# Sparse attention ahead of two routed expert layers: keys on two load queues, the last batch's pooled units ahead of its tiles, a shorter chain behind the last tiles, and first products around the late routing

## The chip, the cores and the metric

One core of a Trainium2 chip. The metric is the device time of one execution in microseconds, the median of several runs. TensorE multiplies, VectorE and ScalarE work on elements, GpSimd fills, adds and issues indirect transfers, SyncE issues plain transfers. In the rows they are PE (PEld: its weight loads), DVE, ACT, POOL and SP; SPq and ACTq are the instructions with which SyncE and ScalarE issue a transfer into their own load queue.

## What is computed

Three stages in a row, all in float32. Attention over 4 batches, 8 heads, 576 positions, head width 64, as the sum of a pooled and a local part:

```python
q_d = q.reshape(B, H, Sd, factor, D).mean(axis=3)          # factor 4; k_d, v_d alike
out_up = np.repeat(sm_attn(q_d, k_d, v_d), factor, axis=2)
mask = np.abs(pos[:, None] - pos[None, :]) < factor        # a band of 7 positions
out_local = np.matmul(softmax(where(mask, scale * q @ k.T, -1e9)), v)
return out_up + out_local
```

Its 2,304 tokens of 512 go through a layer of 8 experts with one expert per token. A skip score decides which tokens are computed (`x @ w_skip > 0`), argmax of `x @ w_gate` picks the expert, and the result is `x + gate * relu(x @ w1[e]) @ w2[e]`. A second layer of 8 experts then takes the two best experts of noisy logits for each token.

## The kernel before

**Layout.** Attention works on 18 tiles of 128 tokens (4.5 per batch, all heads at once). Of a batch's keys one half of the head width lies on partitions 0 to 63 and the other on 64 to 127, `kT[128, 4, 2, S]`, with zeros in the places between, so that one product serves two heads. `load_qk` loads the two halves by two transfers of 64 partitions each and then the queries (128 partitions), all in SyncE's queue. Batch 0 comes in two pieces (positions 0 to 191 for tile 0, then the rest). `load_local` loads a tile's window of values, `vw`, by two transfers of 48 partitions; four window buffers take turns. `load_v` loads a batch's values for pooling.

**Steps.** `push` emits one step of a software pipeline. A step's unit is a local tile (`Local`) or one of five pooled units of a batch (`Pooled`; unit 4 comes first). A step emits the unit's scores and softmax, the transposes (`turn`) of the unit two steps back, then fill work that was scheduled for this step, then the products with the values of the unit three steps back. After these the window of the tile four later is asked for, since its buffer is free. `POOLED` and `PATTERN` say after which tile a batch's pooled units stand: for batch 3 units 4, 0, 1 after tile 12 and units 2, 3 after tile 13.

**The chain behind a tile.** When a batch's pooled outputs are complete, its tiles are finished one per step (`finish`): `load_up` expands the pooled rows into `up` one step later (four buffers), `x_add` adds them to the tile's row `x` at step `ADD` = 3, `x_turn` transposes at `ADD + TURN` (+1), `x_part` multiplies with the routing weights at `ADD + PART` (+3), `x_logits` sums the parts at `ADD + LOGIT` (+5), puts the logits into `lg` and stores the row to `x_d`. Rows `x` have 8 buffers, so the values of tile 8 wait until the row of tile 0 is stored. Steps without a unit follow until the chain of tile 17 is through, 50 steps in all. Additions run on GpSimd, those of tiles 15 and 17 on VectorE.

**Routing of the first layer.** `routing_1(0, TA)` treats tiles 0 to 8 early, a few VectorE steps per `push` (`RS`); `early_2` gives the first expert its tokens, and `ahead1`, a block of 112 tokens of that expert, is gathered as soon as `GA` steps are emitted. `LA` and `LB` say when that expert's two weight matrices (2 MB each) may be asked for. `routing_1(TA, NT)`, the late routing, follows the last logits: counts (`pl.count`), VectorE steps, then `put_1`, a table by which the late tokens' indices are made. Meanwhile TensorE does ahead1's up products (`early_up`, 8 of them with 4 products each, order set by `UA` and `UC`) and, after the capacities, its down products (`ahead1.down`). Then the first block of the expert loop is turned (`ex1[0].turn`), all engines pass a branch, and the loop over experts begins.

**Order.** TensorE, VectorE, ScalarE and GpSimd run in the order in which the program emits their work (`manual_schedule`); SyncE's order in attention is set by a scheduler. In the profile every float32 product has two records on TensorE.

Of the kernel before, what the change touches and what calls it, by code (L numbers as in the profile page):

```python
# [10 lines left out]
F32 = mybir.dt.float32  # L11
# [75 lines left out]
POOLED = (3, 5, 9, 12)  # L87
# [11 lines left out]
def moe_attention_kernel(ctx, tc, q, k, v, w_skip, w_gate, w1, w2, g2, n2, noise, u1, u2, out, dbg=None):  # L99
# [497 lines left out]
    with ExitStack() as actx:  # L597
# [33 lines left out]
        def zero_keys(i, e0, e1, c0=0, c1=S):  # L631
            if c0 == 0:
                kTs.append(shared.tile([128, 4, 2, S], F32, name=f"kT{i}", bufs=1, tag=f"shared{i}"))
            t = kTs[i]
            fill(e0, t[0:64, :, 1, c0:c1])
            fill(e1, t[64:128, :, 0, c0:c1])
# [59 lines left out]
        for d in offsets[0:2]:  # L696
            distances(d)
        mask(offsets[0])
        zero_keys(0, V, P, 0, 192)
        mask(offsets[1])  # L700
        zero_exps(P)
        zero_values(A)
        zero_keys(0, A, P, 192, S)
        zero_exps(P)
        zero_values(A)
        zero_exps(P)
        zero_values(A)
        zero_pooled_keys(0, P, P)

# [12 lines left out]
        def start_2():  # L722
# [4 lines left out]
            nc.gpsimd.dma_start(x_d[0:1], kTs[1][0:1, 0, 1, 0:DM + 16])  # L727
            load_qk(1, 0, S)
# [11 lines left out]
        nc.vector.memset(wall, 0.0)  # L740
        fours = at.tile([128, 32], F32, name="fours", bufs=1)
        nc.vector.tensor_reduce(fours, ident.rearrange("p (c k) -> p c k", k=4), axis=AX.X, op=OP.add)
        nc.vector.tensor_reduce(sel, ident.rearrange("p (k c) -> p c k", k=4), axis=AX.X, op=OP.add)

        qT, qd, vgs, held = {}, {}, {}, {}

        def load_qk(b, c0, c1):

            held["k", b % 2] = b
            if c0 == 0:  # L750
                qT[b] = at.tile([128, 4, S], F32, name="qT", bufs=2)
            for g in range(2):
                r = slice(64 * g, 64 * g + 64)
                nc.sync.dma_start(kTs[b % 2][r, :, g, c0:c1], k[b, r, :, c0:c1])
            nc.sync.dma_start(qT[b][:, :, c0:c1], q[b, :, :, c0:c1])

        def pool_qk(b, n):
# [7 lines left out]
            if n >= 8 and b in ONDVE:  # L765
                for i in range(n - 8, 4, 3):
                    o, x = kd[64:128, i, 1], kT[64:128, i, 1]
                    nc.vector.tensor_reduce(o, x.rearrange("p (g r) -> p g r", r=4), axis=AX.X, op=OP.add)
            elif n < 8:
                i = n // 2  # L770
                o, x = (qd[b][:, i], qT[b][:, i]) if n % 2 == 0 else (kd[0:64, i, 0], kT[0:64, i, 0])
                nc.vector.tensor_reduce(o, x.rearrange("p (g r) -> p g r", r=4), axis=AX.X, op=OP.add)
            else:
                o, x = kd[64:128, :, 1], kT[64:128, :, 1].rearrange("p a (g r) -> p a g r", r=4)
# [141 lines left out]
        class Local:  # L916
# [6 lines left out]
            def scores(self):  # L923
# [5 lines left out]
                for i in range(4):  # L929
                    for s in range(4):  # L930
# [3 lines left out]
                                         kTs[b % 2][:, i, :, ks:ks + W], start=False, stop=True,  # L934
# [129 lines left out]
        def push(unit, *fill):  # L1064
# [46 lines left out]
        load_qk(0, 0, 192)  # L1111
        load_local(0)
        load_qk(0, 192, S)
        for t in range(1, 3):
            load_local(t)
        vgs[0] = load_v(0)

# [7 lines left out]
        for b in range(B):  # L1125
            for i, us in enumerate(PATTERN):
                pooled_after.setdefault(POOLED[b] + i, []).extend((b, u) for u in us)
        for t in range(NT):
            for b in range(B):
                if LOADQK[b] == t:  # L1130
                    load_qk(b, 0, S)
# [37 lines left out]
    run(early_up, UC)  # L1169
# [3 lines left out]
    run(early_up)  # L1173
# [380 lines left out]
    with ExitStack() as mctx:  # L1554
# [11 lines left out]
        ahead1.rooms["yT1"], ex1[0].rooms["xT1"] = (  # L1566
            xp.tile([128, KD, BLK1], F32, name=n, tag="rows2", bufs=5) for n in ("yT0", "xTb"))
# [322 lines left out]
```

## Time and profile before

| | before |
|---|---|
| runs shown | 812.48, 808.34, 814.06 us; median 812.48 |
| profiled execution | 809.09 us, its span 807.2 us |
| TensorE busy | 764.0 us, 95% of the span |
| VectorE, ScalarE, GpSimd busy | 357.1, 259.0, 236.0 us |
| granted TensorE clock, mean | 0.971 |
| moved by DMA | 131.55 MB, 163 GB/s on average |

A time is read in the profile as microseconds from the start of the span. An idle time stands in brackets behind a row of the timeline with what ended it. The granted clock is 1.00 at 2.4 GHz and 0.50 at 1.2 GHz.

### The profile page before, as it was taken

How to read it: one execution, taken by the hardware profiler on the slowest of the kernel's cores; microseconds unless marked ns; L12 is line 12 of the kernel's file. 1: busy time of each engine (PE TensorE's matmuls, PEld its weight loads, DVE VectorE, ACT ScalarE, POOL GpSimd, SP SyncE). 2: the span in 40 equal slices, each digit the busy share in tenths (PEclk: the TensorE clock that was granted, in tenths of full speed). 3: DMA queues.
4: the chain of work that ended last, by engine and by line, in shares of the span. 5: the costliest groups of instructions: out<-in, count | busy, mean ns of one | idle time of the engine just before them, and what ended most of it. 6: DMA issues, size and time to landing. Idle time of an engine off the chain costs nothing.

```text
span 807.2 us, 15233 instructions
## 1 busy us (share of the span) xinstructions
PE 764.0 (95%) x6265; PEld 674.4 (84%) x6265; DVE 357.1 (44%) x814; ACT 259.0 (32%) x492; POOL 236.0 (29%) x243
## 2 busy tenths in 40 slices
PE   4799898799999999998999999999999999999996
PEld 2467576699999999997899899898898898897984
DVE  3896767541111255545975434244243243243210
ACT  6245354211111204322333533234333343343211
POOL 8213513022022253303345502402404305102012
PEclk7999799599999999999999999999999999999999
DMA  9999565869888986234163843724625526424113
GB/s 228 274 260 249 146 172 134 290 160 364 300 304 283 336 312 206 75 87 79 64 170 124 211 128 116 168 80 119 157 67 164 108 83 166 109 79 68 18 14 47
DMA packets 64394, 131.55 MB, mean 163 GB/s; under 512 B 16145, under 2 KB 19232, under 8 KB 63424
## 3 DMA queue, kind: packets, MB, share of 16 engines
q1 hardware_dynamic: 36784, 64.95, 27.8%
q0 software_dynamic: 11984, 25.98, 15.9%
q10 hardware_dynamic: 15552, 39.59, 13.5%
q8 instruction: 52, 0.85, 0.4%
q14 instruction: 22, 0.18, 0.1%
HBM read 101.86 MB, written 23.91 MB: 156 GB/s over the span
## 4 chain that ended last, share of the span: by engine, by line
PE 71%; DMA 2%; issue 2%; DVE 1%; POOL 1%; ACT 0%; POOLq 0%; DVEq 0%; ACTq 0%; SPq 0%
PE pY L1544 26%; PE pH L1529 25%; PE pH L545 8%; PE pY L558 8%; PE pT L1514 2%; PE pT L577 1%; DMA nal<-l_d 1%; PE pT L524 1%; DMA rows<-x_d,ix2g 1%; DMA rows<-x_d,ixrg 1%; PE pT L335 1%; PE pH L566 0%; DMA l_d<-x,ix1w 0%; POOL out L306 0%; PE pH L582 0%
## 5 line engine op out<-in xcount | busy, mean ns | idle before, releaser
L1544 PE MATMUL pY<-w,hh 128*128 128x512 f32 (+6 forms) x640 | 201.0, 395 | 0.0
L1529 PE MATMUL pH<-xh,w 128*128 128x256 f32 (+7 forms) x1024 | 194.8, 302 | 0.0
L1529 PEld LDWEIGHTS pH<-xh,w 128*128 128x128 f32 x1024 | 162.3, 188 | 0.7
L1544 PEld LDWEIGHTS pY<-w,hh 128*128 128x128 f32 (+6 forms) x640 | 114.9, 183 | 26.9
L1205 DVE TENSOR_TENSOR w<-stg,w 128x1024 fp32r<-128x1024 f32 x64 | 82.8, 1299 | 106.7 <-ACT w L1204 106.4
L1544 PE MATMUL pY<-w,hl 128*128 128x512 f32 (+6 forms) x320 | 125.5, 392 | 0.0
L1529 PE MATMUL pH<-xl,w 128*128 128x256 f32 (+7 forms) x512 | 123.1, 301 | 0.0
L1534 DVE SCALAR_TENSOR_TENSOR hl<-pH,hh 128x256 fp32r<-128x256 f32 (+7 forms) x128 | 57.0, 474 | 129.0 <-ACT hh L1533 128.8
L306 POOL DMA_INDIRECT out<-yo,ix2w x35 | 67.6, 1933 | 129.1 <-ACT yo L1546 120.5
L1533 ACT ACTIVATE hh<-pH 128x256 fp32r<-128x256 f32 (+7 forms) x128 | 49.3, 424 | 149.4 <-PE pH L1529 145.5
L1529 PEld LDWEIGHTS pH<-xl,w 128*128 128x128 f32 x512 | 90.0, 188 | 0.0
L301 POOL DMA_INDIRECT rows<-x_d,ix2g x32 | 36.6, 1143 | 155.7 <-PE pT L1514 144.7
L1544 PEld LDWEIGHTS pY<-w,hl 128*128 128x128 f32 (+6 forms) x320 | 58.5, 183 | 15.3
L558 PE MATMUL pY<-hT,w 128*128 128x112 f32 (+7 forms) x512 | 70.9, 300 | 0.0
L1204 ACT ACTIVATE w<-stg 128x1024 fp32r<-128x1024 f32 x64 | 67.1, 1055 | 9.4 <-DMA stg<-in_moe_w 9.2
L558 PEld LDWEIGHTS pY<-hT,w 128*128 128x128 f32 x512 | 69.1, 195 | 0.2
L1546 ACT ACTIVATE yo<-pY,gt 128x512 f32<-128x512 f32 (+6 forms) x35 | 24.1, 688 | 136.7 <-PE pY L1544 76.1
L545 PE MATMUL pH<-xT,w 128*128 128x200 f32 (+6 forms) x448 | 66.2, 301 | 0.0
L545 PEld LDWEIGHTS pH<-xT,w 128*128 128x128 f32 x448 | 61.1, 190 | 1.8 <-issue 1.7
L306 POOL DMA_INDIRECT l_d<-x,ix1w x15 | 14.7, 983 | 92.7 <-DVE x L585 90.3
L560 DVE COPY yT<-pY 128x224 f32<-128x224 f32 (+7 forms) x16 | 7.5, 471 | 71.7 <-PE pY L558 71.7
L976 POOL TENSOR_TENSOR x<-x,up 128x512 f32<-128x512 f32 x16 | 20.2, 1276 | 57.6 <-DMA up<-od 28.4
(408 smaller groups left out, 861.2 us busy)
## 6 DMA issues: line engine op xcount, KB each, us to landing
w<-in_moe_w ACTq DMA_DIRECT2D x16, 2048.0 KB
stg<-in_moe_w SPq DMA_DIRECT2D x64, 512.0 KB, 3.4
vw<-in_v SPq DMA_DIRECT2D x36, 192.0 KB, 4.4
x_d<-x SPq DMA_DIRECT2D x18, 264.0 KB, 3.1
out<-zero ACTq DMA_DIRECT2D x3, 1536.0 KB, 8.5
v<-in_v SPq DMA_DIRECT2D x4, 1024.0 KB, 5.6
up<-od SPq DMA_DIRECT2D x14, 256.0 KB, 4.8
kT<-in_k SPq DMA_DIRECT2D x6, 576.0 KB
```

Source lines behind the costliest of these rows:

```text
L301: return nc.gpsimd.indirect_dma_start(out=dst, out_offset=None, in_=x_d[0:n + 1], in_offset=bass.IndirectOffsetOnAxis(ap=idx, axis=0))
L306: return nc.gpsimd.indirect_dma_start(out=dst, out_offset=bass.IndirectOffsetOnAxis(ap=idx, axis=0), in_=src, in_offset=None, **kw)
L545: nc.tensor.matmul(self.p[:, j], w[:, k, f * 128:(f + 1) * 128], self.xT[:, k], start=k == 0, stop=k == KD - 1)
L558: nc.tensor.matmul(p[:, j], w[:, f, d * 128:(d + 1) * 128], self.hT[:, f], start=f == 0, stop=f == KF - 1)
L976: e.tensor_tensor(xs[t][:, 0:DM], xs[t][:, 0:DM], ups[t], op=OP.add)
L1204: nc.scalar.activation(hi[:, c], st[i], AF.Copy)
L1205: V.tensor_tensor(lo[:, c], st[i], hi[:, c].bitcast(F32), op=OP.subtract)
L1529: nc.tensor.matmul(p, w[:, k, fs], self.x[ch][n][:, k, 0:ch[1] - ch[0]], start=k == 0 and i == 0, stop=k == KD - 1 and i == 2)
L1533: nc.scalar.activation(hi, p, AF.Relu)
L1534: V.scalar_tensor_tensor(lo, p, 0.0, hi.bitcast(F32), op0=OP.max, op1=OP.subtract)
L1544: nc.tensor.matmul(p, h[:, f], w[:, f], start=f == 0 and i == 0, stop=f == KF - 1 and i == 2)
L1546: nc.scalar.activation(o, p, AF.Copy, scale=gate[0:n])
```

## The change

It does six things. (1) The key tile becomes `[128, 2, 4, S]`, so that a half is one run per partition; one half of the keys, and one half of each window, is issued by ScalarE instead of SyncE (4 + 18 transfers). Batch 0 is loaded whole, and the fills with zeros are put in another order. (2) Batch 3's five pooled units all stand after tile 11, ahead of tiles 12 to 17. (3) The expanded rows of tiles 13 to 17 are asked for as soon as these units are through, one per step, and these tiles' additions come one step after `finish` instead of three. (4) `PART` and `LOGIT` go from 3 and 5 to 2 and 3. (5) The early routing's steps are bunched, and gather and weight loads of the first expert are asked for earlier. (6) Four of ahead1's eight up parts stand ahead of the late counts, its first down product ahead of `put_1`, its second behind it.

Counted in steps: tile 0's logits move from step 22 to 20; batch 3's outputs are complete in step 35 instead of 37; the last values stay in step 41, and the last logits move from step 50 to 46. Tile 17's expanded rows are asked for in step 41 (before: 43) and its addition stands in step 43 (before: 45).

```diff
-RS = (3, 3, 1, 0, 6, 3, 0, 0, 3, 3, 3, 1, 3, 3, 3, 3, 3, 3)
+RS = (7, 6, 4, 4, 2, 1, 3, 3, 3, 3, 3, 3)
-UA, UC = 0, 5
-GA, LA, LB, LP, PA = 45, 41, 51, 1, 40
-TURN, PART, LOGIT = 1, 3, 5
+UA, UC = 4, 5
+SWIFT = 13
+GA, LA, LB, LP, PA = 36, 38, 43, 1, 35
+TURN, PART, LOGIT = 1, 2, 3
-POOLED = (3, 5, 9, 12)
+POOLED = (3, 5, 9, 11)
...
-        def load_qk(b, c0, c1):
+        def load_qk(b):
...
-                nc.sync.dma_start(kTs[b % 2][r, :, g, c0:c1], k[b, r, :, c0:c1])
-            nc.sync.dma_start(qT[b][:, :, c0:c1], q[b, :, :, c0:c1])
+                (nc.sync, nc.scalar)[g].dma_start(kTs[b % 2][r, g], k[b, r])
+            nc.sync.dma_start(qT[b], q[b])
...
-                nc.sync.dma_start(vw[64 * g:64 * g + WV, g],
+                (nc.sync, nc.scalar)[g].dma_start(vw[64 * g:64 * g + WV, g],
...
-            else:
+            elif t < SWIFT:
                 schedule(UP, load_up, t)
-            schedule(ADD, x_add, t)
-            schedule(ADD + TURN, x_turn, t)
-            schedule(ADD + PART, x_part, t)
-            schedule(ADD + LOGIT, x_logits, t)
+            add = 1 if t >= SWIFT else ADD
+            schedule(add, x_add, t)
+            schedule(add + TURN, x_turn, t)
+            schedule(add + PART, x_part, t)
+            schedule(add + LOGIT, x_logits, t)
...
                     if un.u == 3:
                         ready.add(un.b)
+                        if un.b == B - 1:
+                            for i, n in enumerate(range(SWIFT, NT)):
+                                schedule(1 + i, load_up, n)
...
-            for i, us in enumerate(PATTERN):
+            for i, us in enumerate(PATTERN if b < B - 1 else (PATTERN[0] + PATTERN[1],)):
...
     run(early_up, UA)
     run(late_1, 8)
-    run(early_up, UC)
+    run(early_up)
+    ahead1.rooms["yT1"], xTb = (xp.tile([128, KD, BLK1], F32, name=n, tag="rows2", bufs=5) for n in ("yT0", "xTb"))
+    ahead1.down(0)
     put_1 = late_1.pop()
     run(mixed(late_1, ranks(place1[1].total, top, order)))
     put_1()
-    run(early_up)
+    ahead1.down(1)
...
     run(capacities(c.caps) + over1.steps + gates + spilled())
-        for d2 in range(KD // 2):
-            ahead1.down(d2)
```

ScalarE at the start, before (`vw`: value windows, `kT`: keys, with zeros filled in by `zcol`, `e`: a tile's scores):

```order
1 L607 ACT_TABLE_LOAD
2 L607 ACTIVATE warm<-warm 128x1
3 L627 ACTIVATE vw_164<-zcol 128x2048
4 L627 ACTIVATE kT_155<-zcol 64x4x384
5 L627 ACTIVATE vw_171<-zcol 128x2048
6 L627 ACTIVATE vw_176<-zcol 128x2048
7 L627 ACTIVATE kT_226<-zcol 64x4x576 x2
8 L947 ACTIVATE e_161<-e_161 128x8x38
```

and now:

```order
2 L608 ACTIVATE warm<-warm 128x1
3 L735 DMA kT_159<-in_k 64x2304
4 L628 ACTIVATE vw_172<-zcol 128x2048
5 L853 DMA vw_172<-in_v 48x1024
6 L628 ACTIVATE vw_179<-zcol 128x2048
7 L853 DMA vw_179<-in_v 48x1024
8 L628 ACTIVATE vw_186<-zcol 128x2048
9 L853 DMA vw_186<-in_v 48x1024
10 L628 ACTIVATE kT_221<-zcol 64x2304 x2
11 L928 ACTIVATE e_169<-e_169 128x8x38
12 L928 ACTIVATE e_176<-e_176 128x8x38
13 L735 DMA kT_221<-in_k 64x2304
```

One half of batch 0's keys is now the first transfer of ScalarE's queue, the windows' halves stand between its fills, and the second half of batch 1's keys waits for two exponentials; the fill of batch 0's keys has left this engine.

SyncE where batch 3's keys and queries are asked for, before (`x_d`: stores of finished rows, the first is tile 0's; `od`, `or`: pooled outputs):

```order
35 L872 DMA vw_176<-in_v 48x1024 x2
36 L754 DMA kT_226<-in_k 64x4x576 x2
37 L755 DMA qT<-in_q 128x2304
38 L872 DMA vw_232<-in_v 48x1024 x2
39 L1000 DMA x_d<-x 128x528
40 L888 DMA up<-or 64x1x128 x4
41 L884 DMA up<-od 64x1x512
```

and now:

```order
33 L869 DMA up<-or 64x1x128 x4
34 L853 DMA vw_186<-in_v 48x1024
35 L735 DMA kT_221<-in_k 64x2304
36 L736 DMA qT<-in_q 128x2304
37 L865 DMA up<-od 64x1x512
38 L981 DMA x_d<-x 128x528
39 L865 DMA up<-od 128x1x512
```

The first store has moved ahead of the window load; one half of the keys has left this queue, and one piece of tile 4's expanded rows stands ahead of the store.

TensorE behind the last logits, before (`xr`: gathered rows, `before`, `onesb`: counts, `wide`: ahead1's rows and hidden layer, `lhs`: the table):

```order
277 L524 MATMUL pT<-ident,xr_186 128x112 x4
278 L216 LDWEIGHTS before
...
301 L212 MATMUL pY<-sel_93,onesb 128x8
302 L545 MATMUL pH<-wide,w_2199 128x112 x20
303 L335 LDWEIGHTS lhs_90
...
320 L335 MATMUL pY<-rt_94,lhs_90 112x32
321 L545 MATMUL pH<-wide,w_2199 128x112 x12
322 L558 MATMUL pY<-wide,w_2346 128x112 x32
323 L524 MATMUL pT<-ident,xr 128x112 x4
```

and now:

```order
278 L525 MATMUL pT<-ident,xr_144 128x112 x4
279 L546 MATMUL pH<-wide,w_2141 128x112 x16
280 L217 LDWEIGHTS before
...
303 L213 MATMUL pY<-sel_93,onesb 128x8
304 L546 MATMUL pH<-wide,w_2141 128x112 x16
305 L559 MATMUL pY<-wide,w_2324 128x112 x16
306 L336 LDWEIGHTS lhs_90
...
323 L336 MATMUL pY<-rt_94,lhs_90 112x32
324 L559 MATMUL pY<-wide,w_2324 128x112 x16
325 L525 MATMUL pT<-ident,xr 128x112 x4
```

The counts moved from ahead of all up products to the middle of them, and the table from between the up products to between the two down products.

## Rows read from the trace of the kernel before

**Rows 1.** Busy time by stage: stretch, its length, engines, clock, DMA share, rate.
```profile
core 0: us, PE busy (x) PEld busy (x) DVE busy (x) ACT busy (x) POOL busy (x), PEclk, DMA share, GB/s
20.00:40.00 20.00, 14.31 (x214) 8.42 (x211) 16.83 (x37) 5.91 (x12) 5.44 (x7) 0.91 1.04 273
60.00:80.00 20.00, 20.00 (x357) 16.13 (x355) 14.27 (x38) 10.22 (x23) 6.76 (x5) 1.00 0.90 250
80.00:100.00 20.00, 16.28 (x192) 10.92 (x195) 13.82 (x33) 7.19 (x19) 10.96 (x8) 0.74 0.62 157
140.00:160.00 20.00, 14.69 (x105) 11.93 (x106) 12.17 (x59) 5.37 (x17) 1.24 (x2) 0.57 0.86 280
500.00:600.00 100.00, 100.00 (x586) 89.93 (x585) 36.34 (x63) 33.51 (x58) 28.93 (x18) 1.00 0.50 125
```
**Rows 2.** The same: batch 2's keys, its queries, the second expert's down weights.
```profile
46.00:50.00 4.00, 3.12 (x79) 2.21 (x74) 3.79 (x11) 0.93 (x2) 0.00 (x0) 1.00 1.05 213
52.00:54.00 2.00, 2.00 (x20) 1.68 (x22) 1.79 (x8) 1.03 (x3) 1.32 (x2) 1.00 0.99 415
186.00:189.00 3.00, 3.00 (x29) 3.00 (x29) 0.39 (x1) 0.00 (x0) 0.00 (x0) 1.00 1.06 393
```
**Rows 3.** Timeline, start: us, length, engine, line, out<-in, count, idle before and releaser.
```profile
6.87 0.73 PE L933 MATMUL pA<-kT,qT 128*32 128x76 f32 x32 [1.60 <-DMA qT<-in_q]
17.72 0.74 DVE L772 TENSOR_REDUCE qd<-qT 128x144 f32<-128x576 f32 x1
27.07 0.68 PE L812 MATMUL pA<-kd,qd 128*32 128x288 f32 x4 [1.74 <-DVE kd L768]
33.61 0.25 DVE L1122 COPY wall<-gates 128x100 f32<-128x100 f32 x1 [2.09 <-DMA gates<-in_moe_w_noise]
35.46 1.38 PE L965 MATMUL pB<-vw,eT 128*32 128x128 f32 x32 [2.50 <-issue]
```
**Rows 4.** Timeline, middle of attention (L784: products that pool the values).
```profile
56.59 1.07 PE L784 MATMUL pT<-v,fours 128*32 128x512 f32 x8 [0.15 <-PE pT L832]
76.95 0.35 SPq L1000 DMA_DIRECT2D x_d<-x  x1
83.19 0.69 DVE L970 TENSOR_TENSOR x<-pB,sums 128x512 f32<-128x512 f32 x1 [5.81 <-DMA x_d<-x]
85.10 0.63 PE L997 MATMUL pW<-sel,xpart 128*128 128x32 f32 x2 [3.72 <-ACT x L999]
85.66 1.94 PE L784 MATMUL pT<-v,fours 128*32 128x512 f32 x8
```
**Rows 5.** Timeline: last values, tile 17's addition, last logits.
```profile
137.07 1.08 PE L965 MATMUL pB<-vw,eT 128*32 128x128 f32 x32
147.18 0.69 DVE L976 TENSOR_TENSOR x<-x,up 128x512 f32<-128x512 f32 x1 [3.73 <-DMA up<-or]
152.96 0.18 DVE L998 COPY lg<-pW 128x25 f32<-128x25 f32 x1 [0.40 <-PE pW L997]
```
**Rows 6.** The page's DMA issues: expanded rows, KB each, us to landing.
```profile
up<-od SPq DMA_DIRECT2D x14, 256.0 KB, 4.8
```
**Rows 7.** Timeline: early gather, late routing, first products.
```profile
148.85 1.08 POOL L301 DMA_INDIRECT xr<-x_d,ix0g  x1 [8.69 <-DVE ix0w L297]
153.64 0.98 PE L524 MATMUL pT<-ident,xr 112*128 112x112 f32 x4 [0.72 <-DMA xr<-x_d,ix0g]
155.35 6.43 PE L545 MATMUL pH<-wide,w 128*128 128x112 f32 x40
162.05 2.91 PE L545 MATMUL pH<-wide,w 128*128 128x112 f32 x24
163.61 0.18 DVE L297 SCALAR_TENSOR_TENSOR ix1w<-rtok,ix1t 112x16 int32<-112x16 f32 x1
165.80 6.30 PE L558 MATMUL pY<-wide,w 128*128 128x112 f32 x55
173.72 5.58 PE L545 MATMUL pH<-xTb,w 128*128 128x112 f32 x48 [1.23 <-PEq L1574]
```

More of the change, by code (lines that the diff above doesn't have):

```diff
@@ L629, in fill, with zero_keys @@
                 e.memset(t, value)
[L631 to L636, printed above, removed]
+        def zero_keys(i, e0, e1):
+            t = shared.tile([128, 2, 4, S], F32, name=f"kT{i}", bufs=1, tag=f"shared{i}")
+            kTs.append(t)
+            fill(e0, t[0:64, 1])
+            fill(e1, t[64:128, 0])
         def zero_pooled_keys(i, e0, e1):
@@ L726, in start_2 @@
             pooled_ones(P)
-            nc.gpsimd.dma_start(x_d[0:1], kTs[1][0:1, 0, 1, 0:DM + 16])
-            load_qk(1, 0, S)
+            nc.gpsimd.dma_start(x_d[0:1], kTs[1][0:1, 1, 0, 0:DM + 16])
+            load_qk(1)
             for n in range(1, NVG):
@@ L737, in start_3 @@
                 mask(d)
-        nc.vector.memset(wall, 0.0)
         fours = at.tile([128, 32], F32, name="fours", bufs=1)
-        nc.vector.tensor_reduce(fours, ident.rearrange("p (c k) -> p c k", k=4), axis=AX.X, op=OP.add)
-        nc.vector.tensor_reduce(sel, ident.rearrange("p (k c) -> p c k", k=4), axis=AX.X, op=OP.add)
         qT, qd, vgs, held = {}, {}, {}, {}
-        def load_qk(b, c0, c1):
+        def load_qk(b):
             held["k", b % 2] = b
-            if c0 == 0:
-                qT[b] = at.tile([128, 4, S], F32, name="qT", bufs=2)
+            qT[b] = at.tile([128, 4, S], F32, name="qT", bufs=2)
             for g in range(2):
                 r = slice(64 * g, 64 * g + 64)
-                nc.sync.dma_start(kTs[b % 2][r, :, g, c0:c1], k[b, r, :, c0:c1])
-            nc.sync.dma_start(qT[b][:, :, c0:c1], q[b, :, :, c0:c1])
+                (nc.sync, nc.scalar)[g].dma_start(kTs[b % 2][r, g], k[b, r])
+            nc.sync.dma_start(qT[b], q[b])
         def pool_qk(b, n):
@@ L933, in scores @@
                         nc.tensor.matmul(p[s * 32:s * 32 + 32, 2 * i:2 * i + 2, :], qT[b][:, i, s0:s0 + 32],
-                                         kTs[b % 2][:, i, :, ks:ks + W], start=False, stop=True,
+                                         kTs[b % 2][:, :, i, ks:ks + W], start=False, stop=True,
                                          tile_position=(0, 32 * s), skip_group_check=True)
@@ L1110, in moe_attention_kernel @@
         vgs = {}
[L1111 to L1114, printed above, removed]
+        for d in offsets[0:2]:
+            distances(d)
+        mask(offsets[0])
+        zero_keys(0, V, P)
+        load_qk(0)
+        mask(offsets[1])
+        for t in range(3):
+            zero_exps(P)
+            zero_values(A)
             load_local(t)
+        zero_pooled_keys(0, P, P)
         vgs[0] = load_v(0)
+        nc.vector.memset(wall, 0.0)
+        nc.vector.tensor_reduce(fours, ident.rearrange("p (c k) -> p c k", k=4), axis=AX.X, op=OP.add)
+        nc.vector.tensor_reduce(sel, ident.rearrange("p (k c) -> p c k", k=4), axis=AX.X, op=OP.add)
         def load_wall():
@@ L1565, in moe_attention_kernel @@
         ahead1.gates = gt1[:, 0:1]
-        ahead1.rooms["yT1"], ex1[0].rooms["xT1"] = (
-            xp.tile([128, KD, BLK1], F32, name=n, tag="rows2", bufs=5) for n in ("yT0", "xTb"))
+        ex1[0].rooms["xT1"] = xTb
         run(capacities(c.caps) + over1.steps + gates + spilled())
-        for d2 in range(KD // 2):
-            ahead1.down(d2)
         ex1[0].turn(0)
```

21 lines of the change are left out of this document (4 added, 17 removed).

## The prediction, made ahead of the run

> **What bounds the kernel now.** I read the busy times by stage first, then the timeline where a stage is not full. In the expert layers TensorE is the bound, 100.00 of 100 us in the stretch shown [rows 1], and nothing there is edited. What the change can move lies ahead of the first product of the expert loop, at 173.72 us [rows 7]. A microsecond saved ahead of that point arrives at the end: the loads behind it are issued relative to it, and TensorE has no idle time there to swallow a shift. In attention TensorE is full from 60 to 80 us, but has only 14.31, 16.28 and 14.69 of 20 us in three weak stages [rows 1]; in the last two the granted clock sinks too, to 0.74 and 0.57, a mixture of the levels 1.2 and 2.4 GHz. Each weak stage has its own cause.
>
> *Start.* Tile 0 begins at 6.87 on its small first load. VectorE starts the pooled sums only at 17.72, behind the scores of later tiles that waited for the rest of the keys; the first pooled product stands behind these sums, 27.07. Then VectorE stands 2.09 us for the gate matrices, which lie behind everything else in SP's queue (33.61); the PSUM bank that it should empty comes late, and TensorE stands 2.50 us, to 35.46 [rows 3].
>
> *Middle.* At 83.19 VectorE has waited 5.81 us for the store of tile 0's row to leave its buffer. That store was issued at 76.95, behind batch 3's keys and queries. TensorE stands 3.72 us and then runs at the lower clock: the same four products take 1.94 us there and 1.07 at 56.59 [rows 4].
>
> *End.* The last values end at 138.15 (137.07 + 1.08), the last logits are copied at 153.13: 15.0 us for a chain of add, turn, part and logits, with a wait of 3.73 for the expanded rows of tile 17 in it [rows 5].
>
> **A, the start: two queues, keys whole.** A half of the keys fills 64 partitions. Such a load moves 213 GB/s; the queries, on 128 partitions, 415; a weight matrix on 128 partitions with runs of 2 KB 393 [rows 2]. So it is the half, not the run of 2,304 bytes, that is slow, and the engines are taken all the same (share 1.05). The new form puts one half in each queue. If they overlap, keys move at about 400, else at 213; no row shows two halves at once, so these are the two ends. I take 400: two halves are 128 partitions.
>
> The Trainium skill says the opposite (DMA: Bandwidth & Descriptors, "Rules for kernel authors"): two transfers to disjoint partition halves serialize, because both spread over all 16 engines. By that, keys would stay at 213. The trace agrees that the engines are all taken during a half; it also shows the same engines moving nearly twice as much for a whole.
>
> Before, tile 0's 0.79 MB were in use at 6.87: about 3.0 us of transfer at 0.26 MB/us (an estimate; the next stage has 273 GB/s [rows 1]) and 3.8 for all else. Now tile 0 needs 2.36 MB: 6.4 us at 0.37 (the first half runs alone for a moment) and 3.8, so it begins at 10.2; with 213 for the keys 5.5 + 2.8 + 3.8, so 12.1. Tile 0 is 3 us later, but tiles 1 and 2 wait no more. Two tiles of scores at some 1.7 us each and VectorE's two short steps for each put the sums at 14.6 instead of 17.72: **-3.1** (serial: -1.0). The gates land earlier by the time saved on two batches of keys, 2.36 MB x (1/0.213 - 1/0.4) = 5.2 us, so 28.4; VectorE wants them at 33.61 - 2.09 - 3.1 = 28.4. The wait goes: **-2.1** (0 to -2.5). The longer fills of zeros cost nothing: they end while the keys are on their way. A = -5.2, ends -1 and -7.
>
> **B, the middle.** Part and logits follow the turn by two and three steps instead of three and five, so tile 0's logits stand in step 20, not 22, and the store leaves the queue behind keys and queries without the two window loads (0.39 MB, about 1.5 us) that stood between. Keys and queries take 6.4 us instead of 1.18/0.213 + 1.18/0.415 = 8.4. The store lands at 83.19 - 1.5 - 2.0 = 79.7, wanted at 77.4 (83.19 - 5.81). VectorE's wait becomes 2.3; TensorE stood 2.1 us less than VectorE, so it hardly stands. That is 3.5, and the lower clock behind it: about 9.4 us of work at half the clock, between 1.94/1.07 for the worst kind and 1.3 for the best, 3.9 us in all, an estimate. 7.4 together; I take **B = -6.5**, since a short stand may remain. Ends -2 and -7.8.
>
> **C, the drain.** With batch 3's five units ahead of tile 12, its outputs are ready in step 35 instead of 37, and the expanded rows of tile 17 are asked for in step 41 instead of 43; the chain ends in step 46 instead of 50. But these rows go into the buffer of tile 14, which GpSimd frees after its adds of tiles 13, 12 and 14 and after the early gather (1.08 [rows 7]) that now stands between them. I put that 1.4 us ahead of the end of the last values, an estimate; five issues take about 3.2 and landing 4.8 [rows 6], so the rows are there 6.6 behind the values. From the add to the last logits it was 5.95 (147.18 to 153.13) with two other tiles between; alone I take 4.1. So 10.7 instead of 15.0, less 1.0 us of turns and parts that TensorE now does ahead of the values: **C = -3.3**. If the rows are not late, -7; if the 2 MB weight load beside them, asked for three steps earlier than now, holds them up, 0.
>
> **D, behind the last logits.** Before: 20 products (6.43 us), the table of late tokens (done by 162.05), 12 more (2.91), the down products (to 172.10), turn and branch (1.62): 20.6 us from 153.13 to 173.72. Now: turn with its copy 1.5, 16 products at the low clock 5.1, counts 0.7, 16 at the high 3.9, half the down products 3.6, then the table 0.6: it ends 15.4 behind the logits, where it ended 8.9 behind. The index work takes 1.7 more (to 163.79) and the gather 4.8 from issue to use (148.85 to 153.64) [rows 7], turn and branch 1.6: 23.5. What hid the gather was 12 products and all of down; now it is half of down. **D = +2.9**; 0 if the gather is quicker than that half, +4.1 if the second 16 products are slow too.
>
> **E, the rest.** ScalarE issues 22 of the loads, each window behind the values that free its buffer. ScalarE is busy 10.22 of 20 us in the full stage [rows 1], and the copy behind such an issue waits for a turn that TensorE does after those values anyway: 0. Routing's steps in bunches (7, 6, 4, 4) and the earlier weight loads: 0, hidden by the scores that TensorE does meanwhile; uncovered, the first bunch is some 2 us of VectorE.
>
> **Sum.** 809.1 - 5.2 - 6.5 - 3.3 + 2.9 = 797.0. The profiled execution took 809.09, its span is 807.2; the median of the runs shown is 812.48 (808.34 to 814.06), so it is one of the quicker ones. I leave the forecast at 797.
>
> **The rivals.**
> *Halves serialize.* Keys stay at 213, as either half has it alone. Then A = -2.0 (sums -1.0, gates -1.0); the store lands at 81.7, TensorE stands 2.2 and the clock sinks in part, B = -2.5: 809.1 - 4.5 - 0.4 = 804.2. For it: share 1.05 at 213. Against it: 415 with the same engines. It is what the rule cited above would make of the change.
> *The tail eats its own gain.* C = 0 and D = +4.1, by the load beside tile 17's rows and a low clock behind it (0.57 now): 801.5.
> *The tail gains.* Rows in time and gather hidden, C = -7, D = 0: 790.4.
> *ScalarE becomes the bound, slower than before.* Each of the 22 loads stands in ScalarE's order; if issue and wait push the copy behind them past TensorE's need, TensorE loses it. The gain of 12.1 is gone at 0.55 us each; at 0.9 it is 809.1 - 12.1 + 19.8 = 816.8. For it: the windows' issue must wait for just-issued products. Against it: half of ScalarE's time is free.
>
> **How the numbers follow.** Forecast 0.46, tail gains 0.10, serial 0.18, tail eats 0.16, ScalarE 0.10. About 1% (8 us) is what a measurement of this kernel can tell from no change. Faster: the first two, half of serial, 0.11 of the tail's loss, 0.76 together; same 0.17; slower 0.07, from ScalarE alone. The range 788 to 807 takes in the tail both ways and the serial case; it leaves out most of ScalarE and the far ends of A and B together. The likeliest case alone: 792 to 801.
>
> **What will show it.** A: first pooled product near 24 us, no gate wait, over 300 GB/s while both halves of the keys run. B: no wait of VectorE over 2.5 us for a store near 75 us, and a clock of 1.00 there. C: last values to last logits near 10.7 us, with VectorE waiting for expanded rows. D: TensorE standing 2 to 3 us ahead of the turn of the first expert's rows. Wrong would be: keys still at 213, a low clock in the middle, or ScalarE's load issues as what TensorE waits for.

## The result, and the profile after

The change makes the kernel slower: 817.71 us in the median of 16 runs against 813.22 for the kernel before in 16 runs beside them. The ratio is 1.0065, with a 95% interval from 1.0042 to 1.0088, so 5.3 us of 813. One run of the change took 1240.02 us at a mean granted clock of 0.571, and the ratio leaves it out. Forecast were 797.0 us, with 788 to 807, which is 12.1 us less than the profiled execution of before.

The two profiled executions differ by more: the span is 819.4 us now and was 807.2. That of after lies 3.7 us above the median of its runs (821.41), that of before 4.1 below (809.09). The traces show where time is lost; how much each part costs is read below from ratios of timed runs.

The stages of after, the columns as in [rows 1]:

```profile
0.00:60.00 60.00, 37.95 (x589) 24.90 (x589) 41.24 (x94) 26.31 (x37) 22.21 (x87) 0.89 0.95 234
...
20.00:40.00 20.00, 12.03 (x195) 7.46 (x199) 15.35 (x31) 5.18 (x12) 6.37 (x28) 0.99 0.90 227
...
60.00:80.00 20.00, 17.54 (x248) 11.82 (x242) 13.59 (x31) 7.24 (x15) 9.65 (x7) 0.83 0.78 196
80.00:100.00 20.00, 18.83 (x286) 13.28 (x285) 13.26 (x34) 9.46 (x25) 8.46 (x6) 1.00 0.99 264
...
180.00:200.00 20.00, 17.28 (x150) 16.82 (x151) 4.76 (x15) 2.70 (x7) 4.01 (x4) 0.85 0.90 284
```

TensorE's first weak stage has become weaker (12.03 of 20 us, 14.31 in [rows 1]). The hole in the middle has moved: 80 to 100 us has 18.83 now at a clock of 1.00, and 60 to 80, which was full, has 17.54 at 0.83. There is a new hole from 180 to 200 us, which belongs to the late part. In the first 60 us the DMA engines are busy for 0.95 of the time.

The start in the timeline of after, the answer to [rows 3]; an engine's name with a q is that engine's issue of a load:

```profile
14.99 0.32 ACTq L853 DMA_DIRECT2D vw<-in_v  x1
15.05 1.24 PE L914 MATMUL pA<-kT,qT 128*32 128x76 f32 x32 [9.78 <-DMA qT<-in_q]
15.36 4.27 ACT L628 ACTIVATE kT<-zcol 64x2304 f32<-64x2304 f32 x2 [6.61 <-DMA qT<-in_q]
18.86 0.74 DVE L753 TENSOR_REDUCE qd<-qT 128x144 f32<-128x576 f32 x1
...
25.86 0.66 PE L793 MATMUL pA<-kd,qd 128*32 128x288 f32 x4
28.21 0.68 PE L793 MATMUL pA<-kd,qd 128*32 128x288 f32 x4 [1.70 <-DVE kd L749]
36.54 0.94 DVE L1118 COPY wall<-gates 128x100 f32<-128x100 f32 x1 [3.89 <-DMA gates<-in_moe_w_noise]
...
39.09 1.69 PE L946 MATMUL pB<-vw,eT 128*32 128x128 f32 x32 [3.23 <-issue]
```

Tile 0 waits until 15.05, not 10.2 as forecast. The sums start at 18.86 (17.72 before, 14.6 forecast), the wait for the gates is 3.89 instead of none, and the fourth tile's values stand at 39.09, 3.6 us later than before. ScalarE does nothing for 6.61 us and takes up its fills right behind the issue of the third window's load.

The prediction read the row at 27.07 in [rows 3] as the first pooled product. It is the second four of them; the first four started at 24.68 in that trace, and start at 25.86 now.

The end of attention and the late part, timeline of after, the answer to [rows 5, 7]:

```profile
147.38 1.66 PE L946 MATMUL pB<-vw,eT 128*32 128x128 f32 x32
156.65 0.18 DVE L979 COPY lg<-pW 128x25 f32<-128x25 f32 x1 [1.51 <-PE pW L978]
...
171.84 0.59 PE L336 MATMUL pY<-rt,lhs 128*112 128x32 bf16 x9 [0.45 <-ACT yT L996]
172.47 0.19 DVE L339 TENSOR_REDUCE tok<-pY 112x16 f32<-112x32 f32 x1 [4.45 <-PE pY L336]
...
172.71 3.83 PE L559 MATMUL pY<-wide,w 128*128 128x112 f32 x32 [0.28 <-DVE tok L339]
...
177.94 0.60 PE L525 MATMUL pT<-ident,xr 112*128 112x112 f32 x4 [1.40 <-DMA xr<-x_d,ix1g]
...
180.70 0.18 DVE L474 TENSOR_TENSOR spill<-code,room1r 128x18 f32<-128x18 f32 x1
...
182.03 0.17 DVE L1601 TENSOR_SCALAR key<-rank 128x8 f32<-128x8 f32 x1 [1.15 <-DVEq L1569]
182.08 7.53 PE L546 MATMUL pH<-xTb,w 128*128 128x112 f32 x48 [3.54 <-DVEq L1569]
```

From last values to last logits it is 7.8 us (149.04 to 156.83) where it was 15.0, but the last values end 10.9 us later. Behind the logits the next rows' first products start at 182.08, 25.3 us on, where it was 20.6. They take 7.53 us for the same 48 rows that took 5.58, and the clock in that stage is 0.85, where it is 1.00 with the old late part (below).

### The profile page after: what moved, and what is told of

Its sections match the earlier page's. It is cut to its first block, busy times and chain, and to the rows that moved or that the text cites. A ratio compares the mean times of both kernels' runs of the same rounds, so it can differ in the third digit from the quotient of the medians.

```text
span 819.4 us, 15250 instructions
## 1 busy us (share of the span) xinstructions
PE 767.6 (94%) x6265; PEld 676.7 (83%) x6265; DVE 362.1 (44%) x814; ACT 257.8 (31%) x491; POOL 237.7 (29%) x242
## 4 chain that ended last, share of the span: by engine, by line
PE 73%; issue 2%; DMA 1%; POOL 1%; DVE 0%; ACT 0%; POOLq 0%; DVEq 0%; ACTq 0%
PE pY L1542 26%; PE pH L1527 24%; PE pH L546 9%; PE pY L559 9%; PE pT L1512 2%; PE pT L578 1%; PE pT L525 1%; DMA rows<-x_d,ix2g 1%; PE pT L336 1%; DMA rows<-x_d,ixrg 1%; PE pH L567 0%; POOL out L307 0%; PE pH L583 0%; PE pT L213 0%; POOL rows L302 0%
## 5 line engine op out<-in xcount | busy, mean ns | idle before, releaser
L1542 PEld LDWEIGHTS pY<-w,hl 128*128 128x128 f32 (+6 forms) x320 | 58.9, 184 | 15.4
```

Of the source, the lines that this page charges most:

```text
L1542: nc.tensor.matmul(p, h[:, f], w[:, f], start=f == 0 and i == 0, stop=f == KF - 1 and i == 2)
```

## The experiments

Each ratio is to runs of the kernel before that stand beside the run. The table's runs come in groups; the version "after, both undone" stands in two of them and the four versions derived from it in a third, so a comparison between these goes by way of the kernel before. A difference of two ratios is called clear of zero when it is larger than its own interval, worked out from the two.

| run | ratio to before | 95% interval |
|---|---|---|
| the change | 1.0065 | 1.0042 to 1.0088 |
| after, old late part | 0.9957 | 0.9933 to 0.9982 |
| before, new late part | 1.0100 | 1.0066 to 1.0135 |
| after, all loads on SyncE | 1.0042 | 1.0015 to 1.0069 |
| before, two queues | 1.0109 | 1.0063 to 1.0155 |
| after, both undone | 0.9937, again 0.9943 | 0.9910 to 0.9965, 0.9919 to 0.9968 |
| the same, table behind the up products | 0.9959 | 0.9927 to 0.9992 |
| the same, keys on ScalarE | 0.9987 | 0.9953 to 1.0020 |
| the same, windows on ScalarE | 0.9985 | 0.9956 to 1.0013 |
| the same, stores and gates apart | 0.9999 | 0.9974 to 1.0023 |
| before, part and logits sooner | 0.9950 | 0.9924 to 0.9976 |
| before, drain's order | 1.0004 | 0.9983 to 1.0025 |
| before, parts two to five | 0.9982 | 0.9957 to 1.0008 |
| before, parts four and five | 0.9978 | 0.9955 to 1.0001 |
| before, parts one (one queue) and four | 0.9922 | 0.9896 to 0.9948 |

### The late part

After, with the late part as it was (`UA` is 0 again, and `UC` 5):

```diff
-    run(early_up)
...
-    ahead1.down(0)
+    run(early_up, UC)
     put_1 = late_1.pop()
     run(mixed(late_1, ranks(place1[1].total, top, order)))
     put_1()
-    ahead1.down(1)
+    run(early_up)
...
     run(capacities(c.caps) + over1.steps + gates + spilled())
+    for d2 in range(KD // 2):
+        ahead1.down(d2)
```

> The changed kernel with the late part put back: the last step of late routing between 20 and 12 of the first products' 32 halves as before, all down products behind the index work. Theory 2 (part six exposes the late table, the gather and the branch): first products of the next rows 20 to 21 us behind the last logits instead of 25, and no low clock behind a stand: 4 to 7 us less than 817.7, so 811 to 814. Theory 1 alone (ScalarE's issues are the whole loss): no change, 816 to 819. Where the chain through routing is the bound whichever products lie beside it: 817.

Measured 0.9957: 0.0108 below the changed kernel, 8.8 us (with both intervals, 6 to 12). The whole loss and more lies here. The reverse edit, part six alone in the kernel before:

> The kernel before with only part six (16 products, counts, 16 products, half the down products, the table, the other half). Theory 2: slower than before by 3 to 6 us, 816 to 819, with TensorE standing for the gathered rows and the branch ahead of the next rows' first products. The prediction's step D: +2.9 (0 to 4.1), 813 to 817. No change, if the index work and the gather ended behind the down products in the kernel before as well: 813.

Measured 1.0100, 8.1 us slower, more than the 6 that were the largest figure expected. TensorE stands as in the changed kernel, and its clock is low behind it:

```profile
176.66 0.61 PE L524 MATMUL pT<-ident,xr 112*128 112x112 f32 x4 [1.41 <-DMA xr<-x_d,ix1g]
180.78 8.11 PE L545 MATMUL pH<-xTb,w 128*128 128x112 f32 x48 [3.51 <-DVEq L1573]
```

The timeline of after with the old late part shows what had been covered:

```profile
162.19 2.91 PE L546 MATMUL pH<-wide,w 128*128 128x112 f32 x24
162.38 0.19 DVE L339 TENSOR_REDUCE tok<-pY 112x16 f32<-112x32 f32 x1 [2.71 <-PE pY L336]
...
164.94 7.31 PE L559 MATMUL pY<-wide,w 128*128 128x112 f32 x64
...
170.57 0.18 DVE L474 TENSOR_TENSOR spill<-code,room1r 128x18 f32<-128x18 f32 x1
...
171.90 0.17 DVE L1602 TENSOR_SCALAR key<-rank 128x8 f32<-128x8 f32 x1 [1.15 <-DVEq L1570]
...
173.31 5.61 PE L546 MATMUL pH<-xTb,w 128*128 128x112 f32 x48 [0.68 <-ACTq L1570]
```

VectorE starts on the table at 162.38 and runs 37 short instructions in a row, to 170.75: indices, capacities, overflow, gates, spills. Its branch comes behind the last one, and it works on from 171.90. TensorE has 2.91 + 7.31 us of products in that time and waits 0.68 us. In the changed kernel the same 37 run from 172.47 to 180.88 and VectorE works on from 182.03, but TensorE has only 3.83 us of products and a turn: it stands 1.40 for the rows and 3.54 for VectorE's branch. The branch is no meeting of all engines. Each takes it in its own order, in the changed kernel at these times (the pair of equal numbers is the start in us; PEldq is TensorE's own):

```profile
L1569 SPq COMPARE_BRANCH  x1: 50/50/50, 176.5 to 176.5; - x1
L1569 POOLq COMPARE_BRANCH  x1: 57/57/57, 176.5 to 176.5; - x1
L1569 PEldq COMPARE_BRANCH  x1: 442/442/442, 178.5 to 178.5; - x1
L1569 ACTq COMPARE_BRANCH  x1: 54/54/54, 178.9 to 178.9; - x1
L1569 DVEq COMPARE_BRANCH  x1: 72/72/72, 181.3 to 181.3; - x1
L1569 DVEq EVENT_SEMAPHORE  x1: 21/21/21, 181.9 to 181.9; - x1
```

SyncE and GpSimd take it 4.8 us ahead of VectorE. TensorE is past it too, but its products behind it start only at 182.08, right after the semaphore that VectorE raises at 181.9, and VectorE comes to its branch only behind its whole list. Behind this stand the clock is lower: 0.85 in the stage above, 1.00 in the same stage of the run with the old late part:

```profile
180.00:200.00 20.00, 19.37 (x161) 18.43 (x160) 3.21 (x9) 2.90 (x7) 5.18 (x6) 1.00 1.04 370
```

A cover in between tells whether this chain sets the price. In the version with both undone (all loads on SyncE and the old late part), one line moves, so that 7.31 us of down products are left behind the table:

```diff
-    put_1()
     run(early_up)
+    put_1()
```

> The version with all loads on SyncE and the old late part (0.9937 of before), with the table of late tokens put behind the last of the 32 first products instead of behind the twentieth: 64 down products (7.31 us) are left to hide what follows the table, where it was 24 first products and these 64 (10.2 us), and half of the 64 (3.83 us) in the changed kernel. VectorE's work from the table's end to the branch was 9.5 us. If that chain is the cost of part six, TensorE stands 2.5 to 3.5 us here: 0.997. If part six cost by the order of the down products or by a lower clock alone, 0.994.

```profile
164.64 7.37 PE L559 MATMUL pY<-wide,w 128*128 128x112 f32 x64 [0.33 <-ACT wide L549]
...
173.95 5.58 PE L546 MATMUL pH<-xTb,w 128*128 128x112 f32 x48 [1.56 <-DVEq L1570]
```

TensorE stands 1.56 us for VectorE's branch, less than expected, and the ratio is 0.9959 beside 0.9937 and 0.9943: 1.5 us, inside its interval, so this step shows in the trace and not in the time. With covers of 10.2, 7.4 and 3.8 us the waits for rows and branch together are 0.68, 1.56 and 4.94 us, and only behind the longest did the 48 rows take 7.53 us instead of 5.6.

### The two queues

After, with every load issued by SyncE:

```diff
-                (nc.sync, nc.scalar)[g].dma_start(kTs[b % 2][r, g], k[b, r])
+                nc.sync.dma_start(kTs[b % 2][r, g], k[b, r])
...
-                (nc.sync, nc.scalar)[g].dma_start(vw[64 * g:64 * g + WV, g],
+                nc.sync.dma_start(vw[64 * g:64 * g + WV, g],
```

> The changed kernel with one edit: the 22 loads that ScalarE issues (a half of the keys, a half of each window) are issued by SyncE again; all else stays. Theory 1 (ScalarE is held at its load issues, which wait for room in its queue, and its copies come late): ScalarE's 6.61 us of idle time ahead of its zero fills and the 3.50 us ahead of an exponential go, the values of the fourth tile start by 36 us instead of 39.09, and the time falls by 4 to 8 us from 817.7, to 810 to 814. Theory 2 (the late part behind the last logits is the whole loss; the queues cost nothing): 817 to 819. Theory 3 (the two queues do bring the keys sooner, as predicted): the start gets later and the time rises, to 820 or more.

Measured 1.0042: 1.9 us less, its interval reaching past zero, where theory 1 had 4 to 8. Tile 0 starts at 12.39 and the fourth tile's values at 36.22. The reverse, the two queues in the kernel before with its old key tile and pieces:

> The kernel before with one edit: ScalarE issues the second half of the keys and of each window, with the old key layout and batch 0 still in two pieces. Theory 1 (ScalarE is held at its issues): slower than before by 3 to 8 us, 816 to 821, with copies of the transposed exponentials late behind load issues. Prediction's step A (two halves overlap, 400 GB/s): the keys of a batch land 2.6 us sooner, the start is shorter, 806 to 810. Halves that share the same engines: no gain in rate, 213 to 270 GB/s while both run, and 812 to 815 if the issues cost nothing.

Measured 1.0109, 8.9 us slower. Its timeline shows ScalarE held at a load:

```profile
21.07 0.66 PE L953 MATMUL pT<-ident,e 128*128 128x128 f32 x4
26.07 0.32 ACTq L872 DMA_DIRECT2D vw<-in_v  x1
26.43 0.60 ACT L956 ACTIVATE eT<-pT 128x512 f32<-128x512 f32 x1 [6.96 <-DMA kT<-in_k]
...
28.90 1.93 PE L965 MATMUL pB<-vw,eT 128*32 128x128 f32 x32
...
86.36 0.35 SPq L1000 DMA_DIRECT2D x_d<-x  x1
...
92.75 0.69 DVE L970 TENSOR_TENSOR x<-pB,sums 128x512 f32<-128x512 f32 x1 [10.81 <-DMA x_d<-x]
```

TensorE turns exponentials at 19.35 and 21.07. ScalarE copies the first turn only at 26.43, 6.96 us after its last work, directly behind the issue at 26.07; the first values follow at 28.90, where they stood at 23.78 before. The profile names the landing of keys as what ended ScalarE's wait; what the issue itself waited for it doesn't show. In the middle VectorE now waits 10.81 us for the store, 5.81 in [rows 4].

Do the halves overlap? With both parts undone the version is the quickest form of the changed kernel itself:

> The changed kernel with both edits of the first two runs: all loads issued by SyncE, and the late part as before. If the two costs are independent, the ratios multiply: 0.9957 x 1.0042 / 1.0065 = 0.993 of the time before, 5 to 6 us faster than before. If ScalarE's issues cost only where the late part exposes them, 0.996 as without this edit. If with the late part hidden again the start decides, below 0.993.

It gave 0.9937, next to the product of the two; 0.996 lies inside its interval too. From it, four loads of keys, then eighteen of windows, go back to ScalarE:

> The version with all loads on SyncE and the old late part (0.9937 of before), with the second half of each batch's keys issued by ScalarE again: four loads. If halves overlap, over 300 GB/s while both run and a start 2 us sooner: 0.991. If they share the same engines at 213 to 270 GB/s, no gain: 0.994 to 0.995; a loss only if the four issues hold ScalarE. The loss of ScalarE's issues by the count (1.9 us over 22 loads in the changed kernel) would give 0.4 us here.

> The same version with the second half of each window issued by ScalarE again: eighteen loads. If the windows' issues hold ScalarE (they wait for room in its queue, or for values that free the buffer), 0.995 to 0.998, with the copies of transposed exponentials late behind them. If the keys' issues are what costs, 0.994 as without this edit.

They gave 0.9987 and 0.9985, each 0.5% above the version without these edits, though both together cost only 0.2% in the changed kernel (0.9957). That version has no run in their group; from the quickest one there, 0.9959, they differ by 0.3%, inside the intervals. So how the cost divides stays open. The traces show that the windows hold up tile 0: it starts at 14.05 with them on ScalarE, and at 12.27 with the keys. The rate is plain. The version's first key halves, all on SyncE, in windows of 2 us (last column GB/s):

```profile
2.00:4.00 2.00, 1.72 (x5) 0.62 (x6) 1.54 (x3) 1.99 (x4) 1.78 (x5) 1.00 1.05 230
4.00:6.00 2.00, 1.27 (x4) 0.26 (x2) 1.97 (x6) 2.00 (x3) 1.88 (x4) 1.00 1.02 226
6.00:8.00 2.00, 0.00 (x0) 0.00 (x0) 0.24 (x1) 2.00 (x2) 1.83 (x6) 1.00 1.00 198
```

and with one half in each queue:

```profile
2.00:4.00 2.00, 1.72 (x5) 0.63 (x6) 1.54 (x3) 1.99 (x4) 1.78 (x5) 1.00 1.01 253
4.00:6.00 2.00, 1.27 (x4) 0.26 (x2) 1.97 (x6) 2.00 (x3) 1.88 (x4) 1.00 0.98 207
6.00:8.00 2.00, 0.00 (x0) 0.00 (x0) 0.23 (x1) 2.00 (x2) 1.83 (x6) 1.00 0.98 203
```

There is no gain to speak of: 221 against 218 GB/s on average, and tile 0 starts at 12.27, within the 12.1 to 12.9 of the versions with all keys and windows on SyncE. The Trainium skill (DMA: Bandwidth & Descriptors, "Rules for kernel authors") says this of disjoint partition halves, from one issuing engine or from two, and the trace agrees.

Do waits in this stretch come from the order in SyncE's queue? Gates (ahead of the first step) and the stores of the tiles' rows (`XQ`) get a queue of their own:

```diff
-XQ = lambda nc: nc.sync
+XQ = lambda nc: nc.scalar
...
+        gates_t = at.tile([128, 25, KD], F32, name="gates", bufs=1)
+        for o, w in ((0, w_gate), (8, w_skip), (9, g2), (17, n2)):
+            nc.scalar.dma_start(gates_t[:, o:o + w.shape[1] // KD, :], w.rearrange("p (e k) -> p e k", k=KD))
...
-                nc.sync.dma_start(t[:, o:o + w.shape[1] // KD, :], w.rearrange("p (e k) -> p e k", k=KD))
...
```

> The version with all loads on SyncE and the old late part (0.9937 of before), with two kinds of small transfers taken out of SyncE's queue: the gate matrices are loaded by ScalarE's queue at the start, and the stores of the tiles' rows leave through ScalarE's queue, which holds nothing else. If these waits (4.16 us for the gates, 2.60 us for a store there) come from what stands ahead in SyncE's queue, both go, and the time falls by 3 to 6 us, to 0.986 to 0.990 of before. If they come from DMA engines that are all taken, whichever queue holds the transfer, the waits stay and the time is 0.994. If ScalarE's store issues hold up its copies, slower than that.

Measured 0.9999: no gain, and 0.6% above 0.9937 and 0.9943. The gates' wait, 4.16 us in the version without this edit, is gone and the fourth tile's values start at 34.04 instead of 36.49. But:

```profile
61.07 0.75 DVE L753 TENSOR_REDUCE qd<-qT 128x144 f32<-128x576 f32 x1 [6.01 <-DMA qT<-in_q]
...
84.31 0.69 DVE L951 TENSOR_TENSOR x<-pB,sums 128x512 f32<-128x512 f32 x1 [2.63 <-DMA x_d<-x]
```

and its first 60 us as a stage:

```profile
0.00:60.00 60.00, 43.18 (x636) 26.01 (x636) 42.26 (x97) 28.38 (x41) 25.28 (x89) 0.86 0.99 246
```

VectorE reaches batch 2's sums 3.9 us sooner and stands 6.01 us for the queries. The store waits 2.63 us in its own queue, 2.60 without the edit. The DMA engines are busy for 0.99 of the first 60 us. So the order in the queue was not what the store waited for. It was what the gates waited for, and the time that they gained was lost at the queries. Why the version is slower stays open: the two edits stand together, and in its first 160 us no wait of ScalarE is put down to a transfer. That the engines' whole load is the bound in the first 60 us fits the share, but no run took bytes away to show it.

### Start, middle and drain, part by part

Part four alone changes two numbers:

```diff
-TURN, PART, LOGIT = 1, 3, 5
+TURN, PART, LOGIT = 1, 2, 3
```

> The kernel before with two numbers changed: part and logits follow the addition's turn after two and three steps instead of three and five. Prediction's step B without the quicker keys: the store of tile 0's row leaves 1.5 us sooner, VectorE waits about 4.3 us for it instead of 5.81, and with the two steps less in the drain 2 to 4 us less time, 0.995 to 0.998. If the store stands in its queue behind the same keys and queries: no change in the middle, and only the drain's two steps, 0 to 2 us. If the earlier logits crowd VectorE or ScalarE: slower by 1 to 3 us.

Measured 0.9950, 4.1 us quicker. From its trace, first the timeline, then the stage:

```profile
85.25 0.69 DVE L970 TENSOR_TENSOR x<-pB,sums 128x512 f32<-128x512 f32 x1 [3.51 <-DMA x_d<-x]
```

```profile
80.00:100.00 20.00, 17.79 (x272) 12.78 (x274) 15.28 (x38) 9.21 (x23) 7.96 (x6) 0.91 0.75 210
```

The wait is 3.51 instead of 5.81 us, the clock 0.91 instead of 0.74, TensorE busy for 17.79 instead of 16.28. From the values of tile 7 to those of tile 10 it takes 21.5 us (78.19 to 99.66) instead of 25.5 (73.83 to 99.32); it is 19.8 to 21.5 in all eight traces with part four and all loads on SyncE, and 24.2 to 25.5 in the three without part four. So 3 to 6 us are gained in the middle. What the two steps less in the drain add the run doesn't separate.

Parts two and three alone (the diff shown ahead, `POOLED`, `SWIFT` and what reads them):

> The kernel before with part two and three alone: batch 3's five pooled units ahead of tile 12, expanded rows of tiles 13 to 17 asked for as soon as these units are done, their addition a step behind. Prediction's step C: 3.3 us less (0 to 7), last values to last logits near 10.7 us instead of 15.0 with VectorE waiting for expanded rows. Rival: the units ahead of tile 12 only move work from behind the last values to ahead of them, so the last logits are no sooner: 0. With routing's steps and the early gather left at their old step numbers a part may be hidden: 0 to -2.

Measured 1.0004. Last values to last logits shrinks to 11.7 us (141.32 to 153.03), but the values end 3.2 us later than before (this trace is 3.2 us behind at tile 9's values already, 81.99 against 78.84), and the early gather, left at its old step, is late: the turn waits 4.06 us for it. Parts two to five together, and four and five without two and three:

> The kernel before with parts two to five alone (batch 3's units together, expanded rows asked for early, part and logits two and three steps behind the addition, routing's steps in bunches): no part of the start and nothing of the late part. Against the run of the changed kernel with all loads on SyncE and the old late part it differs by part one without its queues: batch 0 loaded whole, the key layout, the fills in the new order. If tile 0 waiting to about 12 us instead of 6.9 costs nothing, both are equal within 2 us; if batch 0 whole does bring the pooled sums sooner, this one is 2 to 4 us slower than that one; if tile 0's late start is paid, 2 to 4 us quicker.

> The kernel before with parts four and five: part and logits sooner, routing's steps in bunches of 7, 6, 4, 4, 2, 1 and the weight loads and the gather asked for at lower step numbers; batch 3's units and the expanded rows as before. Part four alone was 0.995, parts two to five together 0.9982. If the bunches cost (VectorE holds tiles of attention back) or the weight load comes in the way of attention's last loads, 0.998; if they cost nothing and it is the reordered units or the early rows, 0.995.

They gave 0.9982 and 0.9978: with the new step numbers too, no gain of parts two and three is measured (0.0004 apart, with an interval of 0.0035). Parts four and five, timeline of the drain:

```profile
132.91 1.08 PE L965 MATMUL pB<-vw,eT 128*32 128x128 f32 x32 [0.85 <-ACT eT L956]
...
149.74 0.18 DVE L998 COPY lg<-pW 128x25 f32<-128x25 f32 x1 [1.98 <-PE pW L997]
```

and with two and three as well:

```profile
139.89 1.88 PE L966 MATMUL pB<-vw,eT 128*32 128x128 f32 x32
...
150.25 0.18 DVE L999 COPY lg<-pW 128x25 f32<-128x25 f32 x1 [1.67 <-PE pW L998]
```

The distance falls from 15.9 to 8.7 us, and the values end 7.8 us later (133.99, 141.77). Of these, 3.8 us are there at tile 9's values already (79.20, 83.04), which stand ahead of batch 3's units. Counted from these values, the last ones end 50.9 to 54.8 us on in the three traces with part four and without parts two and three, and 58.7 to 63.4 in the five with parts two to four and all loads on SyncE. The last logits come 67.5 to 70.7 us on without the two parts, and 67.4 to 73.1 with them. The work has moved from behind the last values to ahead of them, and the logits are no sooner. Part five seems to take back some of part four's gain: 0.9978 against 0.9950, 2.3 us, with an interval that reaches zero.

Last, part one with one queue beside part four, and the version with both undone again as its reference:

> The kernel before with part one without its second queue (batch 0 loaded whole, key layout, fills reordered, all loads on SyncE) and part four (part and logits two and three steps behind the turn); no reordered batch 3, no early rows, no bunches of routing, the old late part. If the gains add up (part four alone 0.995, part one 0.9937 / 0.9982 = 0.9955), 0.9905: 803 to 804. If part one's 0.45% was measuring noise, 0.995. If parts two, three and five are needed for it, 0.995 to 0.998.

> The changed kernel with all loads on SyncE and the old late part a second time, as the reference of the two others on the same chip: 0.9937 (0.991 to 0.9965) before. If the run without parts two, three and five is as quick or quicker than this one, these three parts bring nothing here; if this one is quicker by over 2 us, they do.

0.9922 and 0.9943. The first is the quickest of all, 6.3 us less than before, with none of parts two, three, five and six. Against part four alone (0.9950) part one with one queue brings 2.3 us; against parts two to five (0.9982 to 0.9940) it brought 3.4; only the second difference stands clear of its interval.

## Why the prediction was wrong, step by step

**D, the late part, is the step that failed most.** It put the table 15.4 us behind the logits; it stood at 15.6 (172.43). From there it counted 1.7 for the indices, 4.8 for the gather and 1.6 for turn and branch, 8.1 in all, because it followed the rows alone. The products behind the branch also wait until VectorE has passed it, and VectorE has everything queued ahead of it to finish first: 9.65 us from the table to the products, 172.43 to 182.08. The step asked what had hidden the gather, and not what had hidden the rest of VectorE's list. And it priced no low clock behind the stand: 1.95 us on the next 48 rows. By the traces with the new and the old late part it is 25.3 against 19.9 us from the last logits (156.83 to 182.08, 153.46 to 173.31) and 1.9 of clock, 7.3 us in all; the runs say 8.8, and 8.1 for the reverse edit. Forecast were 2.9, with 4.1 as the upper end.

**A, the start.** The value of 400 GB/s was the wrong end of its bounds; the serial end was right, as the rival and the cited rule had it. For that end the prediction gave tile 0 at 12.1 and a gain of 2.0 us: with one queue tile 0 starts between 12.1 and 12.9 in the six profiles that have this start and all keys and windows on SyncE, and part one brings 2.3 to 3.4 us, the smaller of them not clear of zero. The sums do start sooner by what that end says, at 15.9 to 16.7, but the gates' wait, which should have shrunk by 1.0, is 4.16 to 4.37 us with one queue against 2.01 to 3.57 in six traces with the old start. The fourth tile's values start at 35.9 to 36.5 with one queue and at 35.1 to 38.3 in those six. So it is in part luck that the number agrees with 2.0, and where part one gains the traces do not show.

**E, the second queue, was not free.** The argument that a window's load waits for work that ScalarE needs anyway holds for later windows. The first three wait for no values, and ScalarE stood 6.61 us until the third one was issued. The loss is 8.9 us in the kernel before, 0.4 us for each of its 23 loads there; in the changed kernel it is 1.4 to 1.9, not clear of zero. The rival had 0.9 for each load and put its break-even at 0.55: its mechanism was right in the kernel before, and its price too high. It was not what made this kernel slower.

**B, the middle, was right in kind and too large.** Part four alone gives 4.1 us, drain and all, where 6.5 were taken for the middle (2 to 7.8), and 3 to 6 us of it are seen there. The wait shrank to 3.51, not 2.3, since the quicker keys did not come. In the changed kernel it was 3.51 too, and 6.99 in the run with the old late part.

**C, the drain.** The chain behind the last values did shrink: forecast were 10.7 us, and it is 7.8 in the changed kernel and 8.7 to 13.1 in the five traces with parts two to four and all loads on SyncE. The step that failed is the 1.0 us allowed for work that TensorE now does ahead of the values: counted from tile 9's values, the last ones end 7.6 us later on average (52.8, 60.3). C is 0, which is the end of its range, but not through the weight load that the prediction gave as the reason for that end.

**Part five** was put at nothing, with 2 us if uncovered; the runs lean to 2.3, not clear of zero.

**The sum of the runs**: part one with one queue -2.3 to -3.4, second queue +1.4 to +1.9, part four -4.1, parts two and three 0, part five +2.3, late part +8.8. That is 5.0 to 6.6, beside 5.3 measured. Several terms are differences of the same runs, so this shows only that they are consistent. The forecast had three gains and one loss: two gains came at half to two thirds of their size, the third was not there, and the loss was three times what it was put at.

## What to carry to other kernels

Ahead of moving work that covers a chain, list everything that the chain's last wait needs on every engine, not only the operand that comes last on its own path: work behind a branch can wait until another engine has passed it, and that engine passes it only behind its whole queue (here 9.65 us from the table to the products). Shortening the distance between two events gains nothing if the first one moves back by as much, so measure both ends from the start. Where the DMA engines were taken for nearly all of a stretch, a better place in the queue moved the wait to another transfer and a second queue brought no rate, and a load issue on an engine that also computes can hold its next copy for microseconds.

## What the runs showed of the hardware

Two key halves at once moved at 203 to 253 GB/s, 221 on average; one after the other they moved at 198 to 230, 218 on average. A load's issue on ScalarE held its next copy for 6.96 us. Behind 4.94 us of waiting, TensorE ran 48 rows in 7.53 us that take 5.6 at a granted clock of 1.00. The five engines took one branch at times from 176.5 to 181.3 us, and TensorE's products behind it waited for the last of them, VectorE. Equal programs drift apart in the drain: the version with both parts undone and the one with the table moved behind the up products are the same up to the last logits, and these start at 147.85 in one trace and at 152.15 in the other, so a difference of 4 us between two traces proves nothing there.
